# Retention, a top-1 mixture of experts and a rational feed-forward block on one core: the counts are copied sooner, the transition to the first expert and the last four blocks are written in another order

## The chip, the cores and the metric

One core of a Trainium2 chip. TensorE (PE) multiplies, and its weight loads are shown as an engine of their own (PEld); VectorE (DVE), ScalarE (ACT) and GpSimd (POOL) work element by element; SyncE (SP) and POOL issue transfers. Each engine takes its instructions in order and waits on semaphores. The metric is the device time of one execution, in microseconds (us).

## What is computed

```python
for t in range(S):                      # B=2, H=8, S=768, D=64
    state = gamma * state + k[:, :, t] (outer) v[:, :, t]
    y[:, :, t] = scale * q[:, :, t] @ state
x = y as 1536 tokens of 512
logits = x @ w_gate                     # 8 experts
e = argmax(logits); gate = softmax(logits)[e]
# tokens in order take the slots of their expert, up to its capacity (384)
y = gate * relu(x @ w1[e]) @ w2[e]      # 512 -> 1024 -> 512
h = y @ w_in                            # 512 -> 2048
g = (a0 + a1 h + a2 h^2 + a3 h^3) / (1 + |b0||h| + |b1|h^2 + 1e-6)
out = g @ w_out                         # 2048 -> 512
```

## The kernel before

**Precision.** All large products are split: an operand is a rounded high part (`whi`, `xh`, `ht[0]`, `gh`) and the rest (`wlo`, `xl`, `ht[1]`, `gl`), and a product is three matmuls: high by high, low by high, high by low. The high part of a weight is written by ACT (`split_hi`, L143), the low part by DVE (`split_lo`, L148), both on half tiles of 128x1024 whose raw form has six buffers.

**Attention** (`attention`) runs over twelve units of 128 tokens. In unit u PE computes the scores of u+1 (`scores`), the part of u's output that comes from the state (`inter`), the part from the unit itself (`intra`), the new state (`state`) and the logits of u-1 (`gate_mm`); DVE masks the scores (`mask`, tile `scm`), scales the output (`attn_xt`) and, by the tables `LO_AT` and `LO_END`, makes low parts of the first expert's weights. The units fall into two groups, 0 to 6 and 7 to 11. After a group's last unit `gate_parts`, `rank_mm`, `rank_pos` and `rank_put` find each token's expert and slot; `place_mm` (L490) then turns the tiles `pe` and `rr` by matmul into a table `tab` of token numbers by slot, from which POOL gathers rows of x (`xg`). The first group is placed in unit 10, and the first 128 rows of expert 0 are gathered there at once (`early_gather`, transposed in `early_x` as `xtp`).

**The transition** (`attn_tail`): the first layer of expert 0 on those 128 rows (`win_l1`, two halves of twelve products, both in one tile of two PSUM banks), relu by ACT (`win_relu`), transposes back (`win_turn`, tile `htp`), their high and low parts (`win_parts`, tile `ht`), and in between the second group's routing, its `place_mm` and `counts`, which copies the tokens per expert from PSUM (`off<-rk`, L499) and tests for an overfull expert. Attention's PSUM pool closes there and a new one opens: the first product of the second layer (`win_l2`, L754, in `first_expert`) waits until everything that reads the old pool is done. `first_expert` runs the second layer's 24 products with the transposes of the next 96 rows (`expert_x`, L882) after the 18th.

**Experts 1 to 7** follow in `moe`, then `ffn`: 48 steps n, each a block of 128 hidden features by 512 tokens. `ffn_a` multiplies, ACT, DVE and POOL compute the fraction (`ffn_i`, `ffn_p`, `ffn_r`, `ffn_e`), `ffn_g` splits it (low part by POOL, for n = 47 by DVE), `ffn_b` multiplies it out into four tiles m of 128 tokens. After the last of a row of blocks DVE adds the tiles to `acc` (`ffn_out`, L1122) and POOL scatters finished tiles to the output (`put_out`, L1131). `ffn_tail` writes this out for the last blocks, n = 44 to 47: one row of four tiles ends with block 43, the last one with block 47.

The order is written by hand (manual schedule): an engine's queue holds its instructions as the code calls them.

Of the kernel before, what the change touches and what calls it, by code (L numbers as in the profile page):

```python
# [34 lines left out]
WA, WC = 7, 3  # L35
LOADS = (0, 1, 0, 1, 0, 1, 0, 2, 1, 1, 1, 2)
HI_AT = {4: (0,), 5: (1,), 8: (2,), 9: (3, 4), 10: (5,)}
LO_AT = {5: (0,), 6: (1,)}
LO_END = {9: (2,), 10: (3,), 11: (4,)}
NA = 48  # L40
LOAD_AT = {1: (34, 0), 2: (34, 1), 6: (35, 0), 7: (35, 1)}
# [39 lines left out]
class Build:  # L81
# [398 lines left out]
        tt(out=pe, in0=self.over(self.col("iota"), g), in1=self.across(pm, g, 128), op=ALU.is_equal)  # L480
        self.place[b] = (pe, rr)

    def place_mm(self, b, tag="tpa"):
        nc = self.nc
        pe, rr = self.place.pop(b)
        u0, u1 = self.units(b)
        n = E * (self.nsub + 1)
        tp = self.bank(tag, "tp")[:, 0 : 2 * n]
        for i in range(u1 - u0):
            nc.tensor.matmul(tp, lhsT=pe[:, i], rhs=rr[:, i], start=(i == 0), stop=(i == u1 - u0 - 1))  # L490
        tp = tp.rearrange("p (a n) -> p a n", a=2)
        if b == 0:
            nc.vector.tensor_copy(self.tab, tp)
        else:
            nc.vector.tensor_tensor(out=self.tab, in0=self.tab, in1=tp, op=ALU.add)

    def counts(self):
        nc = self.nc
        nc.vector.tensor_copy(self.off, self.cnt)  # L499
        nc.vector.tensor_tensor(out=self.off[:, 0:1], in0=self.off[:, 0:1], in1=self.pad, op=ALU.add)  # L500
        nc.vector.tensor_reduce(out=self.ovf, in_=self.off[0:1, 0:E], axis=AX.X, op=ALU.max)
        top = float(min(W, self.cap))
        nc.vector.tensor_scalar(out=self.ovi, in0=self.ovf, scalar1=top, scalar2=None, op0=ALU.is_gt)
        nc.vector.tensor_scalar(out=self.ov, in0=self.ovf, scalar1=top, scalar2=None, op0=ALU.is_gt)
# [52 lines left out]
    def attention(self):  # L557
        nc, tc, a = self.nc, self.tc, self.a
        with ExitStack() as st:
# [42 lines left out]
            for u in range(NU):  # L602
                last = u == NU - 1
                if u + 4 < NU:
                    for c in range(2):
                        self.attn_load(u + 4, c)
                self.load_next(LOADS[u])
                if u + 2 < NU:
                    self.scale(u + 2, pool)
                if u + 3 < UPB:  # L610
                    self.y_table(u + 3, pool)
                for n in LO_AT.get(u, ()):
                    self.split_lo(n // 2, n % 2)
                if 1 < u < NU - 1:
                    self.scores(u + 1)
                    self.mask(u + 1)
                if u - 4 in done:
                    self.place_mm(done[u - 4])
                if u == UA + 3:
                    self.early_gather()  # L620
                if u - 2 in done:
                    next(gate)
                self.inter(u)
                self.intra(u)
                self.attn_xt(u)
                if u - 2 in done:
                    next(gate)
                if u == 1:
                    self.scores(2)
                    self.mask(2)  # L630
                self.state(u)
                if u == 0:
                    self.scores(1)
                    self.mask(1)
                    nc.scalar.activation(out=self.wi[:, :, 0:128], in_=ident, func=AF.Copy)
                    nc.scalar.activation(out=self.wi[:, :, 128:], in_=wg, func=AF.Copy)
                if u == 1:
                    nc.scalar.activation(out=self.tri, in_=self.col("tri"), func=AF.Copy)
                    nc.scalar.activation(out=self.b0a, in_=self.ab[:, 4:5], func=AF.Abs)
                    nc.scalar.activation(out=self.b1a, in_=self.ab[:, 5:6], func=AF.Abs)  # L640
                    nc.vector.memset(self.cq, 1.0 + 1e-6)
                if u - 2 in done and not last:
                    self.rank_mm(done[u - 2])
                if last:
                    self.early_x()
                if u:
                    self.gate_mm(u - 1)
                    self.gate_out(u - 1, (0,))
                if u - 1 in done:
                    gate = self.gate_parts(done[u - 1])  # L650
                    next(gate)
                if u:
                    self.gate_out(u - 1, (1,))
                for n in HI_AT.get(u, ()):
                    self.split_hi(n // 2, n % 2)
                if u - 2 in done and not last:
                    self.rank_pos(done[u - 2])
                if u - 3 in done and not last:
                    self.rank_put(done[u - 3])
                for n in LO_END.get(u, ()):  # L660
                    self.split_lo(n // 2, n % 2)
# [19 lines left out]
    def attn_tail(self):  # L681
        u, b = NU - 1, len(GROUPS) - 2
        self.gate_mm(u)
        ps = self.pair_bank("s", "l1").rearrange("p (a n) -> p a n", a=2)
        ps = [ps[:, 0], ps[:, 1]]
        self.early_lo()
        self.win_l1(self.x0, ps, range(0, 10))
        self.gate_group(b)
        self.gate_out(u)
        self.load_next(4)  # L690
        self.rank_mm(b)
        self.rank_pos(b)
        self.h0 = self.wp.tile([128, 2, 512], F32, tag="wt", name="h0", bufs=3)
        self.split_hi(3, 0)
        self.win_l1(self.x0, ps, range(10, 12))
        self.win_relu(ps, self.h0, 0)
        self.split_hi(3, 1)
        self.rank_put(b)
        self.win_l1(self.x0, ps, range(12, 20))
        tp = self.win_turn(self.h0, 0, self.bank("xk", "htp"))  # L700
        self.win_l1(self.x0, ps, range(20, 24))
        self.win_relu(ps, self.h0, 1)
        self.split_lo(2, 1)
        t1 = self.win_turn(self.h0, 1, self.bank("st", "htp"))
        self.place_mm(b, "lg")
        self.indices(self.gidx, E * (self.nsub + 1))
        self.ht0 = self.win_parts(tp)
        self.split_lo(3, 0)
        self.ht1 = self.win_parts(t1)
        self.split_lo(3, 1)  # L710
        self.counts()
        self.nprep = 8

    def win_l1(self, x, ps, seq):
# [75 lines left out]
    def first_expert(self):  # L790
        bank = self.bank
        acc, hts = bank("l2"), (self.ht0, self.ht1)
        seq = [(0, i) for i in (0, 3, 6, 9, 1, 4, 7, 10, 2, 5, 8, 11)]
        seq += [(1, i) for i in (0, 3, 6, 9, 1, 4, 2, 5, 8, 11, 7, 10)]
        self.win_l2(hts, acc, seq[:18], last=False)
        self.expert_x(0, 1)
        self.rows()
        self.win_l2(hts, acc, seq[18:], first=False)
        y = self.y_rows(acc, 0)
        x = [t.pop(0)[:, :, 128:W] for t in (self.xh, self.xl)]  # L800
        ps = [bank("l1")[0:W2] for _ in range(2)]
        h = self.wp.tile([128, 2, 512], F32, tag="wt", name="h1", bufs=3)[0:W2]
        self.win_l1(x, ps, range(0, 12))
        self.win_relu(ps, h, 0)
        self.x_gate(1, 0)
        self.win_l1(x, ps, range(12, 18))
        self.y_turn(y, 0)
        ht0 = self.win_split(h, 0, bank("l1"))
        self.x_gate(1, 1)
        self.win_l1(x, ps, range(18, 24))  # L810
        self.win_relu(ps, h, 1)
        self.expert_x(1, 0)
        self.gather(4)
        self.prep_next()
        acc = bank("l2")
        self.win_l2((ht0,), acc, [(0, i) for i in range(0, 6)], last=False)
        ht1 = self.win_split(h, 1, bank("l1"))
        self.win_l2((ht0,), acc, [(0, i) for i in range(6, 12)], first=False, last=False)
        self.prep_next()
        self.expert_x(1, 1)  # L820
        self.gather(5)
        for _ in range(2):
            self.prep_next()
        self.win_l2((ht0, ht1), acc, [(1, i) for i in range(12)], first=False)
        self.y0 = self.y_rows(acc, 1)
        for _ in range(2):
            self.prep_next()
        for i in range(4):
            del self.whi[i], self.wlo[i]
# [356 lines left out]
    def ffn_tail(self):  # L1186
# [6 lines left out]
        self.ffn_b([(n - 4, m) for m in range(4)])  # L1193
        self.ffn_r(n)
        self.ffn_e(n - 1)
        self.ffn_g(n - 1)
        self.ffn_out()
        self.put_outs()
        self.ffn_e(n)
        self.ffn_g(n)  # L1200
        self.ffn_b([(k, m) for k in (n - 3, n - 2) for m in range(4)])
        for m in ((n - 1, 0), (n - 1, 1), (n, 0), (n, 1)), ((n - 1, 2), (n, 2)), ((n - 1, 3), (n, 3)):
            self.ffn_b(m)
            self.ffn_out()
            self.put_outs()

# [110 lines left out]
```

## Time and profile before

| | |
|---|---|
| median of 3 runs | 524.83 us (524.3 to 525.09) |
| the profiled execution | 523.4 us, of which 521.6 us are the span from the first to the last instruction |
| PE busy | 504.5 us, 97% of the span, 3538 matmuls |
| PEld, DVE, ACT, POOL busy | 442.1, 404.4, 361.7, 244.9 us |
| PE's share of the chain that ended last | 62% |
| mean granted clock | 0.989 of full speed |

The page divides the span into 40 slices of 13 us with the busy share of each engine in tenths and the clock that was granted to PE (PEclk); the timeline lists instructions with start, duration and, in square brackets, the idle time of their engine ahead of them and what ended it. A row that merges several instructions spans them all.

### The profile page before, as it was taken

Reading aid. Unit: us, or ns where it says so; the run is one execution under the profiler, and the core shown is the slowest. Engines: PE = TensorE matmul, PEld = TensorE weight load, DVE = VectorE, ACT = ScalarE, POOL = GpSimd, SP = SyncE. Lnnn points to the kernel's source line nnn. Section 1 sums busy time; section 2 is a strip of 40 time slices with the busy share of each in tenths; the row PEclk is TensorE's granted clock in tenths of the full one; section 3 lists DMA queues with packets and bytes.
Section 4 is the critical chain, followed back from the end, with each engine's and each line's share of the span. In section 5 each row is a group of like instructions: output and inputs, shape, how many; then the busy total and the mean of one; then the engine's idle time right before and its main releaser. Section 6 shows DMA issues by size and latency. Waiting matters only on the chain.

```text
span 521.6 us, 9409 instructions
## 1 busy us (share of the span) xinstructions
PE 504.5 (97%) x3538; PEld 442.1 (85%) x3538; DVE 404.4 (78%) x577; ACT 361.7 (69%) x588; POOL 244.9 (47%) x187
## 2 busy tenths in 40 slices
PE   7999969999999999999999999999999999999994
PEld 5888747999999999999978888888888888888873
DVE  3468752887977979787496989999899998865972
ACT  1345514886685957764697989999899987776750
POOL 2531031113432548163345446775667865444765
PEclk9999989999999999999999999999999999999998
DMA  8999752789987999995220002222022200000203
GB/s 316 402 416 352 218 169 78 244 311 311 325 284 254 363 279 334 277 263 194 72 90 1 0 1 81 82 80 81 1 80 83 80 1 0 1 0 0 82 4 158
DMA packets 27266, 83.08 MB, mean 159 GB/s; under 512 B 4944, under 2 KB 5328, under 8 KB 27216
## 3 DMA queue, kind: packets, MB, share of 16 engines
q1 hardware_dynamic: 24592, 75.09, 42.6%
q0 software_dynamic: 2624, 7.35, 4.0%
q8 instruction: 28, 0.46, 0.4%
q14 instruction: 22, 0.18, 0.1%
HBM read 71.93 MB, written 10.49 MB: 158 GB/s over the span
## 4 chain that ended last, share of the span: by engine, by line
PE 62%; issue 2%; POOL 1%; ACT 1%; DVE 1%; POOLq 0%; ACTq 0%
PE h L1029 8%; PE h L1031 8%; PE h L1030 8%; PE o L1102 7%; PE o L1100 7%; PE o L1101 7%; PE l L911 3%; PE l L913 3%; PE l L912 3%; PE l L940 3%; PE l L939 3%; PE l L938 3%; POOL out L1131 1%; PE tp L882 1%; ACT fh L1060 0%
## 5 line engine op out<-in xcount | busy, mean ns | idle before, releaser
L148 DVE TENSOR_TENSOR wlo<-raw,whi 128x1024 fp32r<-128x1024 f32 x80 | 110.8, 1399 | 17.3 <-ACT whi L143 17.0
L1080 POOL TENSOR_TENSOR gg<-fx,gg 128x512 fp32r<-128x512 f32 x47 | 61.1, 1299 | 70.8 <-issue 62.9
L143 ACT ACTIVATE whi<-raw 128x1024 fp32r<-128x1024 f32 x80 | 83.1, 1053 | 3.5 <-PE l L939 3.4
L1029 PE MATMUL h<-yh,whi 128*128 128x512 f32 x192 | 74.9, 390 | 0.4 <-DVE fx L1068 0.4
L1100 PE MATMUL o<-whi,gg 128*128 128x512 f32 x192 | 74.8, 390 | 0.0
L1031 PE MATMUL h<-yh,wlo 128*128 128x512 f32 x192 | 74.8, 389 | 0.0
L1030 PE MATMUL h<-yl,whi 128*128 128x512 f32 x192 | 74.7, 389 | 0.0
L1101 PE MATMUL o<-wlo,gg 128*128 128x512 f32 x192 | 74.7, 389 | 0.0
L1102 PE MATMUL o<-whi,gg 128*128 128x512 f32 x192 | 74.7, 389 | 0.0
L1055 POOL TENSOR_TENSOR fw<-fh,fw 128x512 f32<-128x512 f32 x48 | 64.3, 1339 | 15.3 <-ACT fw L1044 14.5
L204 POOL TENSOR_TENSOR gq<-gq 128x512 int32<-128x512 int32 x16 | 26.1, 1629 | 85.9 <-DVE gq L201 68.2
L1042 ACT ACTIVATE fx<-h,ct 128x512 f32<-128x512 f32 x48 | 37.3, 777 | 39.4 <-PE h L1031 37.6
L911 PE MATMUL l<-xh,whi 128*128 128x224 f32 x224 | 62.0, 277 | 0.1
L938 PE MATMUL l<-hh,whi 128*128 128x224 f32 x224 | 61.9, 276 | 0.0
L913 PE MATMUL l<-xh,wlo 128*128 128x224 f32 x224 | 61.5, 275 | 0.0
L940 PE MATMUL l<-hh,wlo 128*128 128x224 f32 x224 | 61.5, 274 | 0.0
L912 PE MATMUL l<-xl,whi 128*128 128x224 f32 x224 | 61.5, 274 | 0.0
L939 PE MATMUL l<-hl,whi 128*128 128x224 f32 x224 | 61.4, 274 | 0.0
L1066 DVE SCALAR_TENSOR_TENSOR fw<-fw,cq,h 128x512 f32<-128x512 f32 x48 | 35.6, 741 | 10.0 <-ACT h L1061 10.0
L911 PEld LDWEIGHTS l<-xh,whi 128*128 128x128 f32 x224 | 43.0, 192 | 0.4 <-ACT yh L777 0.3
L939 PEld LDWEIGHTS l<-hl,whi 128*128 128x128 f32 x224 | 43.0, 192 | 0.1
L938 PEld LDWEIGHTS l<-hh,whi 128*128 128x128 f32 x224 | 43.0, 192 | 0.1
(161 smaller groups left out, 1184.5 us busy)
## 6 DMA issues: line engine op xcount, KB each, us to landing
raw<-wm SPq DMA_DIRECT2D x64, 512.0 KB
r<-wf SPq DMA_DIRECT2D x32, 512.0 KB
kv<-kv SPq DMA_DIRECT2D x24, 512.0 KB
wd<-gq SPq DMA_DIRECT2D x16, 256.0 KB
raw<-wd SPq DMA_DIRECT2D x8, 512.0 KB
xd<-xs SPq DMA_DIRECT2D x12, 256.0 KB
ca<-ct SPq DMA_DIRECT2D x1, 268.0 KB
xg<-xd,gidx POOLq DMA_INDIRECT x16
```

The source lines that it names most:

```text
L143: nc.scalar.activation(out=self.whi[i][:, sl], in_=raw, func=AF.Copy)
L148: (eng or self.nc.vector).tensor_tensor(out=self.wlo[i][:, sl], in0=raw, in1=self.whi[i][:, sl].bitcast(F32), op=ALU.subtract)
L911: nc.tensor.matmul(ps[:, fi], lhsT=wh[:, sl], rhs=xh[:, k], start=(k == 0), stop=False)
L912: nc.tensor.matmul(ps[:, fi], lhsT=wh[:, sl], rhs=xl[:, k], start=False, stop=False)
L938: mm(lhsT=wh[:, ws], rhs=fh, start=(f == 0 and o % 2 == 0), stop=False)
L939: mm(lhsT=wh[:, ws], rhs=fo, start=False, stop=False)
L1029: nc.tensor.matmul(h, lhsT=wh[:, sl], rhs=self.yh[:, k, ts], start=(k == 0), stop=False)
L1030: nc.tensor.matmul(h, lhsT=wh[:, sl], rhs=self.yl[:, k, ts], start=False, stop=False)
L1031: nc.tensor.matmul(h, lhsT=wl[:, sl], rhs=self.yh[:, k, ts], start=False, stop=(k == 3))
L1100: self.nc.tensor.matmul(ps, lhsT=gh[:, ms], rhs=wh[:, ws], start=first, stop=False)
L1101: self.nc.tensor.matmul(ps, lhsT=gh[:, ms], rhs=wl[:, ws], start=False, stop=False)
L1102: self.nc.tensor.matmul(ps, lhsT=gl[:, ms], rhs=wh[:, ws], start=False, stop=last)
```

## The change

No operation is added or dropped; POOL and DVE, PE and the PSUM banks meet in another order.

- Units: the low parts of the first two half tiles are made in units 6 and 7, not 5 and 6 (`LO_AT`); in unit 10 the state's part of the output (`inter`) goes ahead of `place_mm`.
- Transition: the second half of the first layer has a bank of its own (`xk`); `counts` is divided into `count` (the copy, right after `rank_put`) and `overfull`; `place_mm` moves ahead of the last four products of the first layer, into the bank pair `y`; the transposes of both halves follow each other behind these products.
- First expert: the 96 rows' transposes stand after 14 products, not 18.
- End: of the four sums and scatters of the row that ends with block 43, two sums and one scatter go ahead of block 46's split, the others between block 47's steps; the last two blocks are multiplied tile by tile.

```diff
-LO_AT = {5: (0,), 6: (1,)}
+LO_AT = {6: (0,), 7: (1,)}
...
-    def place_mm(self, b, tag="tpa"):
+    def place_mm(self, b, tp=None):
...
-        tp = self.bank(tag, "tp")[:, 0 : 2 * n]
+        tp = (self.bank("tpa", "tp") if tp is None else tp)[:, 0 : 2 * n]
...
-    def counts(self):
-        nc = self.nc
-        nc.vector.tensor_copy(self.off, self.cnt)
+    def count(self):
+        self.nc.vector.tensor_copy(self.off, self.cnt)
+
+    def overfull(self):
+        nc = self.nc
         nc.vector.tensor_tensor(out=self.off[:, 0:1], in0=self.off[:, 0:1], in1=self.pad, op=ALU.add)
...
+                if u - 2 in done:
+                    next(gate)
+                self.inter(u)
                 if u - 4 in done:
                     self.place_mm(done[u - 4])
                 if u == UA + 3:
                     self.early_gather()
-                if u - 2 in done:
-                    next(gate)
-                self.inter(u)
                 self.intra(u)
...
-        ps = self.pair_bank("s", "l1").rearrange("p (a n) -> p a n", a=2)
-        ps = [ps[:, 0], ps[:, 1]]
+        ps = [self.pair_bank("s", "l1")[:, 0:512], self.bank("xk", "l1")]
...
         self.rank_put(b)
+        self.count()
+        self.split_lo(2, 1)
         self.win_l1(self.x0, ps, range(12, 20))
-        tp = self.win_turn(self.h0, 0, self.bank("xk", "htp"))
+        self.place_mm(b, self.pair_bank("y", "tp"))
         self.win_l1(self.x0, ps, range(20, 24))
         self.win_relu(ps, self.h0, 1)
-        self.split_lo(2, 1)
+        t0 = self.win_turn(self.h0, 0, self.bank("lg", "htp"))
         t1 = self.win_turn(self.h0, 1, self.bank("st", "htp"))
-        self.place_mm(b, "lg")
         self.indices(self.gidx, E * (self.nsub + 1))
-        self.ht0 = self.win_parts(tp)
         self.split_lo(3, 0)
+        self.ht0 = self.win_parts(t0)
+        self.split_lo(3, 1)
         self.ht1 = self.win_parts(t1)
-        self.split_lo(3, 1)
-        self.counts()
+        self.overfull()
...
-        self.win_l2(hts, acc, seq[:18], last=False)
+        self.win_l2(hts, acc, seq[:14], last=False)
         self.expert_x(0, 1)
         self.rows()
-        self.win_l2(hts, acc, seq[18:], first=False)
+        self.win_l2(hts, acc, seq[14:], first=False)
...
         self.ffn_e(n - 1)
+        self.ffn_out(2)
+        self.put_out(self.outs.pop(0))
         self.ffn_g(n - 1)
-        self.ffn_out()
+        self.ffn_e(n)
+        self.ffn_out(1)
+        self.ffn_g(n)
+        self.ffn_out(1)
         self.put_outs()
-        self.ffn_e(n)
-        self.ffn_g(n)
         self.ffn_b([(k, m) for k in (n - 3, n - 2) for m in range(4)])
-        for m in ((n - 1, 0), (n - 1, 1), (n, 0), (n, 1)), ((n - 1, 2), (n, 2)), ((n - 1, 3), (n, 3)):
-            self.ffn_b(m)
+        for m in range(4):
+            self.ffn_b([(n - 1, m), (n, m)])
```

What stands in DVE's queue from the second group's `pe` on, in `attn_tail`; `wlo` are low parts of weights, `ht` the low parts of the first layer's output, `off<-rk` the copy of the counts. Before:

```order
L480 TENSOR_TENSOR pe<-ct,pm 128x640
L148 TENSOR_TENSOR wlo<-raw,whi 128x1024
L495 TENSOR_TENSOR tab<-tab,tp 128x64
L508 TENSOR_SCALAR gidx<-tab 128x32
L745 TENSOR_TENSOR ht<-htp,ht 128x512
L148 TENSOR_TENSOR wlo<-raw,whi 128x1024
L745 TENSOR_TENSOR ht<-htp,ht 128x512
L148 TENSOR_TENSOR wlo<-raw,whi 128x1024
L499 COPY off<-rk 128x16
```

and after:

```order
L480 TENSOR_TENSOR pe<-ct,pm 128x640
L498 COPY off<-rk 128x16
L148 TENSOR_TENSOR wlo<-raw,whi 128x1024
L495 TENSOR_TENSOR tab<-tab,tp 128x64
L510 TENSOR_SCALAR gidx<-tab 128x32
L148 TENSOR_TENSOR wlo<-raw,whi 128x1024
L747 TENSOR_TENSOR ht<-htp,ht 128x512
L148 TENSOR_TENSOR wlo<-raw,whi 128x1024
L747 TENSOR_TENSOR ht<-htp,ht 128x512
```

The copy went from the end of the row to its second place, and the last operation of the row that reads the old PSUM pool is now the second `ht`.

PE's queue at the same place, from the last product of the first layer's first 20 to the transposes of the next rows (`tp<-ct,xg`); `tp<-rr,pe` is `place_mm`. Before:

```order
L719 MATMUL l_889<-wlo,xh_111 128x512
L738 MATMUL htp<-ct,h_969 128x128 x4
L719 MATMUL l_889<-whi,xl_112 128x512 x4
L738 MATMUL htp<-ct,h_969 128x128 x4
L490 MATMUL tp<-rr,pe 128x64 x5
L754 MATMUL l_1057<-whi,ht 128x512 x4
L754 MATMUL l_1057<-wlo,ht 128x512 x4
L754 MATMUL l_1057<-whi,ht 128x512 x8
L754 MATMUL l_1057<-wlo,ht 128x512 x2
L882 MATMUL tp<-ct,xg 128x128 x4
```

and after:

```order
L721 MATMUL l_890<-wlo,xh_111 128x512
L490 MATMUL tp<-rr,pe 128x64 x5
L721 MATMUL l_890<-whi,xl_112 128x512 x4
L740 MATMUL htp<-ct,h_970 128x128 x8
L756 MATMUL l_1058<-whi,ht 128x512 x4
L756 MATMUL l_1058<-wlo,ht 128x512 x4
L756 MATMUL l_1058<-whi,ht 128x512 x6
L884 MATMUL tp<-ct,xg 128x128 x4
```

`place_mm` moved ahead of the last four products of the first layer and both halves' transposes stand behind them; the next rows' transposes moved four products ahead. (The trace lists ten matmuls for `place_mm`'s five.)

POOL's queue at the end, block 45's and 46's low parts (`gg`), block 47's denominator (`fw`) and the scatters (`out`). Before:

```order
L1080 TENSOR_TENSOR gg<-fx,gg 128x512
L1055 TENSOR_TENSOR fw<-fh,fw 128x512
L1080 TENSOR_TENSOR gg<-fx,gg 128x512 x2
L1131 DMA out<-acc_4022,perm 1536x512
L1131 DMA out<-acc_4024,perm 1536x512
```

and after:

```order
L1082 TENSOR_TENSOR gg<-fx,gg 128x512
L1057 TENSOR_TENSOR fw<-fh,fw 128x512
L1082 TENSOR_TENSOR gg<-fx,gg 128x512
L1133 DMA out<-acc_4023,perm 1536x512
L1082 TENSOR_TENSOR gg<-fx,gg 128x512
L1133 DMA out<-acc_4025,perm 1536x512
```

The first of the eight scatters moved ahead of block 46's low part.

## Rows read from the trace of the kernel before

**Rows 1.** The page: the granted clock in 40 slices of the span.

```profile
PEclk9999989999999999999999999999999999999998
```

**Rows 2.** Stretches: length, then PE, PEld, DVE, ACT, POOL busy, clock, DMA.

```profile
60.00:80.00 20.00, 14.21 (x75) 10.96 (x74) 11.15 (x39) 5.32 (x12) 4.43 (x4) 0.83 0.68 219
...
300.00:400.00 100.00, 100.00 (x443) 82.81 (x442) 92.73 (x130) 92.56 (x147) 65.40 (x49) 1.00 0.20 64
```

**Rows 3.** Timeline of the units: start, duration, what, idle before and its releaser.

```profile
32.51 1.16 PE L331 MATMUL sc<-kv 64*128 64x128 f32 x16 [0.32 <-DVE scm L294]
...
51.21 1.77 PE L490 MATMUL tp<-rr,pe 128*128 128x64 f32 x14 [0.51 <-DVE pe L480]
...
52.92 0.67 PE L331 MATMUL yt<-kv,s 64*64 64x128 f32 x16
...
54.03 1.20 POOL L832 DMA_INDIRECT xg<-xd,gidx  x1 [7.31 <-DVE gidx L508]
...
57.75 0.66 PE L673 MATMUL xtp<-ct,xg 128*128 128x128 f32 x4
```

**Rows 4.** Waits of the weight loads, 20 to 55 us: total, times, longest.

```profile
PEld sc L331 <- DVE scm L294: 0.8, 2, 0.5
```

**Rows 5.** A stretch behind the early gather, columns as in rows 2.

```profile
57.00:57.25 0.25, 0.25 (x10) 0.25 (x8) 0.00 (x0) 0.25 (x1) 0.00 (x0) 1.00 0.10 33
```

**Rows 6.** Timeline of the transition, 64 to 82 us.

```profile
64.66 0.50 PE L719 MATMUL l<-whi,xh 128*128 128x512 f32 x1 [0.69 <-ACT h L728]
...
65.72 0.82 DVE L480 TENSOR_TENSOR pe<-ct,pm 128x640 f32<-128x640 f32 x1
...
66.98 1.18 PE L719 MATMUL l<-whi,xl 128*128 128x512 f32 x4
...
68.84 0.66 PE L738 MATMUL htp<-ct,h 128*128 128x128 f32 x4 [0.69 <-ACT h L728]
69.34 1.23 PE L490 MATMUL tp<-rr,pe 128*128 128x64 f32 x10
69.54 0.60 ACT L744 ACTIVATE ht<-htp 128x512 fp32r<-128x512 f32 x1 [0.26 <-PE htp L738]
...
71.32 1.00 POOL L832 DMA_INDIRECT xg<-xd,gidx  x1 [16.08 <-DVE gidx L508]
71.55 1.22 DVE L148 TENSOR_TENSOR wlo<-raw,whi 128x1024 fp32r<-128x1024 f32 x1
...
72.68 0.68 DVE L745 TENSOR_TENSOR ht<-htp,ht 128x512 fp32r<-128x512 f32 x1
...
74.42 0.17 DVE L499 COPY off<-rk 128x16 f32<-128x16 f32 x1
...
74.73 2.05 PE L754 MATMUL l<-whi,ht 128*128 128x512 f32 x4 [4.17 <-DVE off L499]
...
81.35 0.60 PE L882 MATMUL tp<-ct,xg 128*128 128x128 f32 x4
```

**Rows 7.** Stretches around the lower clock, columns as in rows 2.

```profile
73.00:74.00 1.00, 0.00 (x0) 0.00 (x0) 1.00 (x2) 0.00 (x0) 0.70 (x2) 0.55 0.82 270
...
79.00:80.00 1.00, 1.00 (x4) 0.74 (x4) 0.00 (x0) 0.00 (x0) 0.00 (x0) 0.54 0.85 328
...
516.00:517.00 1.00, 0.00 (x0) 0.00 (x0) 0.00 (x0) 0.00 (x0) 0.69 (x2) 0.91 0.38 156
```

**Rows 8.** Timeline of the end.

```profile
504.10 2.48 DVE L1122 TENSOR_TENSOR acc<-o,acc 128x512 f32<-128x512 f32 x4
...
505.46 1.30 POOL L1080 TENSOR_TENSOR gg<-fx,gg 128x512 fp32r<-128x512 f32 x1 [0.83 <-ACT gg L1078]
...
509.09 0.39 PE L1100 MATMUL o<-whi,gg 128*128 128x512 f32 x1
...
514.73 0.69 DVE L1122 TENSOR_TENSOR acc<-o,acc 128x512 f32<-128x512 f32 x1 [0.67 <-PE o L1102]
...
516.39 0.98 POOL L1131 DMA_INDIRECT out<-acc,perm  x1 [0.31 <-issue]
```

## The prediction

> **What bounds the kernel now.** I first read the granted clock over the span: one slice near 70 us and the last one are below full [rows 1]. The stretches say where PE, which carries the chain, is not busy: from 300 to 400 us it works all the time, 443 matmuls in 100 us or 0.23 us each, but from 60 to 80 us it works 14.2 of 20 us, at 0.83 of the clock [rows 2]. So the span is PE's queue, and only places where PE waits, runs slow, or has already ended can give time. The timeline names them. In the units PE waits 0.32 us for a mask and 0.51 us for `pe` [rows 3]. In the transition it stands 4.17 us, until the copy of the counts is done [rows 6]; then the clock is at half, 1.2 of 2.4 GHz: 73 to 74 us has a mean of 0.55, so it fell at 73.1, and 79 to 80 has 0.54, so it rose at 79.9 [rows 7]. At the end PE is done before 514.7, but POOL issues the last scatter only at 516.39 [rows 8].
>
> **The units (0.9 us).** The first `wlo` no longer stands ahead of a mask in DVE's queue. PE gets back 0.32 us [rows 3] for certain; the weight loads show two waits for masks, 0.8 us together [rows 4], partly beside running matmuls. Between 0.3 and 0.8 I take 0.4, near PE's own row. The moved `wlo` find their high parts ready and stand between masks that DVE has time for; if it had not, the same 0.3 would return a unit later.
> `inter` now goes ahead of `place_mm`. PE's 0.51 us wait for `pe` is covered by these 0.67 us of products [rows 3], which need only the state: 0.5, or 0.25 if DVE's own chain to `pe` does not come forward with PE.
> What is late next is the early gather. Its index waits for `place_mm`, which starts only some 0.3 us sooner, while PE arrives at `xtp` 0.9 sooner than 57.75 [rows 3]. But the transfers are nearly silent from 57.0 on [rows 5], so its bytes were in about 0.7 us before they were used; 0.3 sooner, it is in at 56.7, and PE comes at 56.85. So 0.9 stands; the lower bound, a late landing signal, is 0.3.
>
> **The transition (2.1 us).** I use before's times; all of it moves forward by the 0.9. DVE ends `pe` at 65.72 + 0.82 = 66.54. With the second bank PE need not wait for the relu (0.69 at 64.66), but that gives nothing: its eight products then end at 64.66 - 0.69 + 8 x 0.23 = 65.8, and `place_mm` needs `pe`. So PE waits 0.8 us and runs `place_mm` from 66.6, 1.23 us, to 67.8, and the four products, 1.18, to 69.0. The relu, an ACT operation of 0.60, ends at 69.6; the first half's transposes run meanwhile, the second half's then take 0.66, to 70.3. There PE runs out of work.
> DVE has copied the counts (0.17), made one `wlo` (1.22, to 67.9), then the table, the index and the second `wlo`, all before 70. The first `ht` waits for ACT's high part, 69.6 + 0.60 = 70.2; then 0.68, a third `wlo` of 1.22, and the second `ht` of 0.68: 72.8. Such rows overlap by 0.1 (71.55 + 1.22 against the next start, 72.68), so 72.5. That `ht` is now the last reader of the old PSUM pool; with the 0.14 us from copy to product (74.42 + 0.17 to 74.73) PE starts the second layer at 72.65, not 74.73: 2.1 us, 1.8 without overlaps (all durations [rows 6]). The count's copy itself costs nothing now: the third `wlo` and `ht` stand where it stood, and they set the end.
> The transposes after 14 products need the gathered rows. The gather was issued 0.75 us after `place_mm` (70.57 to 71.32), so now at 68.6; PE comes at 72.65 + 14 x 0.23 = 75.9, 7.3 us later. Before it was 10.0 us (71.32 to 81.35), the early gather took at most 3.7 (54.03 to 57.75) [rows 3, 6]. I take no wait; at worst it is 2.7. Behind them ten products, 2.3 us, hide ACT's and DVE's split of those rows; before, six did, without a wait.
>
> **The clock (0.8 us).** In before PE worked at half speed from 74.73 to 79.9 [rows 6, 7], 5.2 us, which cost 2.6. The new stand is 70.3 to 72.65, 2.35 us. The clock fell 2.5 us after PE had stopped (69.34 + 1.23 = 70.6, to 73.1), and at the end of the kernel 2.1 us after the last product: 516 to 517 has 0.91, a fall at 516.8, with the last matmul over by 514.7 [rows 7, 8]. So 2.35 us is just where it falls. The gain lies between 0 (it falls and costs as much) and 2.6 (it stays). I take that it falls and costs 1.8, so 0.8: nearer to the row of before, less one third because the stand is shorter.
>
> **The end (0.65 us).** POOL had been idle 0.83 us ahead of block 46's `gg` at 505.46 [rows 8]; the first scatter takes that place, once its sum is there (504.1 + 2.48/4 = 504.7). `gg` then ends at about 507.3 instead of 506.8; PE needs it at the third product of 509.09, 509.5, so 2.2 us cover the move. Two sums are now behind block 47's three DVE operations and one on each side of its split; their banks are not needed again, and block 47's fraction is ready 1.2 us (two sums of 0.62) sooner. The products tile by tile do not change PE's end. POOL's queue then has a free place for every scatter: the last one waits for the last sum, 514.73 + 0.69 = 515.42, and with the 0.31 us that stands ahead of a transfer in its row starts at 515.7, not 516.39: 0.65, between 0.4 and 0.75. Its landing is as long as before.
>
> **The sum.** 0.9 + 2.1 + 0.8 + 0.65 = 4.45 us. The profiled execution took 523.4 us, 1.8 outside its span of 521.6; the sum makes 519.0 of it. The median is 524.83, and there I put it: 520.4. After the transition PE has no further wait that this would open: the experts' weights are fetched as their buffers come free, and these come free as much sooner.
>
> **Rivals.** *The clock stays up.* For it: PE's other waits, up to 0.69 us [rows 6], left the clock alone, and 2.35 is less than the 2.5 of before. Against it: the 2.1 us at the end. The sum is then 0.9 + 2.1 + 2.6 + 0.65 = 6.25: 518.6. The Trainium skill ("TensorE: Matmul & The Clock Gate", section "Why this matters for your kernels") says that only longer idle gaps between bursts of matmuls throw the clock back, and by that rule this rival would hold; the fall at the end of this trace speaks against leaning on it.
> *It falls for as long as before.* The half-speed stretch of 73.1 to 79.9 was 6.8 us, of which PE stood 1.6; if all 6.8 meet products they cost 3.4. Then the clock gives 0 to -0.8: 521.2 to 522.0. A wait for the gathered rows would end there too.
> *The change does not do what it says:* another reader of the old pool is as late as the copy was. Units and end remain, 1.55: 523.3. Against it: the order has no later reader than the second `ht`.
> *Slower.* PE's new wait for `pe`, 0.8 us, lowers the clock already there, ahead of `place_mm`. It decides if such a wait is enough; 0.69 was not. Then `place_mm`, four products and eight transposes, 1.23 + 1.18 + 2 x 0.66 = 3.7 us, take 3.7 more, and with the second stand behind them the half clock costs 3.4 instead of 2.6: 0.9 + 2.1 - 3.7 - 0.8 + 0.65 = -0.85, 525.7.
>
> **How the numbers follow.** Forecast 520.4 (519.5 to 521.1): 50%. Clock stays, 518.6: 31%. Longer half clock or a gather wait, 521.2 to 522.0: 12%. No effect in the transition, 523.3: 4%. Slower, 525.7: 3%. The range takes the first three with their bounds, 518.1 to 522.0, and leaves out the last two and the edges. A measurement of this kernel tells 0.2%, 1.05 us, from no change: the first three cases and most of the fourth are faster by more (0.95); the slower case at 525.7 is within it or just beyond: 0.03 same, 0.02 slower.
>
> **What would show it.** In the trace after: no wait of PE for DVE's copy, but one of about 2.4 us for the second `ht`, at 71.7 in its own time; the second layer's products 0.9 + 2.1 us sooner; a wait of about 0.8 us for `pe` ahead of `place_mm`; no wait for a mask near 32 us; `xtp` at about 56.9. The stretches tell whether the clock fell, near 72, and for how long: that alone moves the result by 2 us. At the end, one scatter ahead of `gg` and the last one 0.3 us behind the last sum. I am wrong if PE waits for the gathered rows, if POOL's `gg` comes after 509.5, or if the weights of expert 1 now come late.

## The result and the profile after

| | before | after |
|---|---|---|
| median | 524.57 us (523.14 to 526.71, 8 runs) | 519.54 us (518.2 to 522.71, 8 runs) |
| the profiled execution | 523.4 us, span 521.6 | 519.17 us, span 517.4 |
| mean granted clock of it | 0.989 | 0.999 |

The ratio is 0.9905 (95% interval 0.988 to 0.9931): 5.0 us faster, forecast 4.45. The time lies between the forecast, 520.4, and its first rival, 518.6. In the profiled execution the clock did not fall in the transition, as in the rival. The page's line of granted clock after, where before had two slices below full [rows 1]:

```profile
PEclk9999999999999999999999999999999999999999
```

The transition after (PE and POOL; start, duration, engine, line, and in brackets the wait and what ended it; rows of before are in [rows 6]):

```profile
60.96 0.48 PE L721 MATMUL l<-whi,xh 128*128 128x512 f32 x1
...
67.62 1.30 PE L490 MATMUL tp<-rr,pe 128*128 128x64 f32 x10 [0.85 <-DVE off L498]
...
70.60 0.66 PE L740 MATMUL htp<-ct,h 128*128 128x128 f32 x4 [0.25 <-ACT h L730]
73.55 1.21 PE L756 MATMUL l<-whi,ht 128*128 128x512 f32 x4 [2.29 <-DVE ht L747]
...
76.90 0.60 PE L884 MATMUL tp<-ct,xg 128*128 128x128 f32 x4
...
79.66 0.39 PE L721 MATMUL l<-whi,xh 128*96 128x512 f32 x1
```
```profile
69.31 1.22 DVE L148 TENSOR_TENSOR wlo<-raw,whi 128x1024 fp32r<-128x1024 f32 x1
...
69.68 1.73 POOL L834 DMA_INDIRECT xg<-xd,gidx  x1 [13.44 <-DVE gidx L510]
```

PE waits 0.85 us ahead of `place_mm` (the releaser shown is DVE's copy, which ends just behind `pe`), and 2.29 for the second `ht`, where before it stood 4.17 for the copy. It comes to the gathered rows 7.2 us after their issue and does not wait. The first `xk` starts 1.02 us later than in the trace of before, which has the earliest start of all fourteen traces of this document (27.16 to 28.45). The two traces at that place, at the first group's routing and (before) at three more rows that the table below starts from, before and then after:

```profile
27.16 1.19 PE L350 MATMUL xk<-wi,xt 128*128 128x136 f32 x8
42.18 0.22 DVE L387 TENSOR_TENSOR eq<-eq,ct 128x56 f32<-128x56 f32 x1
43.96 0.19 PE L422 MATMUL rk<-oh,tri 128*128 128x56 bf16 x1
...
60.01 0.48 PE L719 MATMUL l<-whi,xh 128*128 128x512 f32 x1
...
83.18 0.39 PE L719 MATMUL l<-whi,xh 128*96 128x512 f32 x1
...
514.30 0.39 PE L1102 MATMUL o<-whi,gg 128*128 128x512 f32 x1
```
```profile
28.18 1.19 PE L350 MATMUL xk<-wi,xt 128*128 128x136 f32 x8
42.48 1.07 POOL L264 TENSOR_TENSOR kv<-kv,ca 128x512 f32<-128x512 f32 x1 [3.71 <-PE sc L331]
42.68 0.94 DVE L387 TENSOR_TENSOR eq<-eq,ct 128x56 f32<-128x56 f32 x1
45.18 0.19 PE L422 MATMUL rk<-oh,tri 128*128 128x56 bf16 x1 [0.78 <-DVE oh L390]
52.45 1.77 PE L490 MATMUL tp<-rr,pe 128*128 128x64 f32 x14
58.72 0.63 PE L675 MATMUL xtp<-ct,xg 128*128 128x128 f32 x4 [0.15 <-PE yt L331]
```

Neither the wait for a mask nor that for `pe` is there any more [rows 3], but a new one of 0.78 us ahead of `rk`: DVE's `eq`, 0.22 us long before, took 0.94 while POOL worked on `kv`. The end after (before: [rows 8]):

```profile
501.53 1.00 POOL L1133 DMA_INDIRECT out<-acc,perm  x1 [0.43 <-DVE acc L1124]
502.56 1.31 POOL L1082 TENSOR_TENSOR gg<-fx,gg 128x512 fp32r<-128x512 f32 x1
...
511.19 0.69 DVE L1124 TENSOR_TENSOR acc<-o,acc 128x512 f32<-128x512 f32 x1 [0.67 <-PE o L1104]
512.16 0.98 POOL L1133 DMA_INDIRECT out<-acc,perm  x1 [0.38 <-DVE acc L1124]
```
```profile
510.77 0.39 PE L1104 MATMUL o<-whi,gg 128*128 128x512 f32 x1
```

The last scatter now starts 1.39 us after PE's last product began and waits for the last sum; before that was 516.39 - 514.30 = 2.09 us.

The 4.2 us between the two spans add up stage by stage, each as the change of a distance between two rows:

| stretch | before | after | gain |
|---|---|---|---|
| start to first `xk` | 27.16 | 28.18 | -1.02 |
| to `xtp` (units) | 30.59 | 30.54 | 0.05; without the 0.78 for `rk` 0.83 |
| to the first layer's first product | 2.26 | 2.24 | 0.02 |
| to the second layer's first product | 14.72 | 12.59 | 2.13 |
| to the first product of the 96 rows (clock) | 8.45 | 6.11 | 2.34 |
| to PE's last product | 431.12 | 431.11 | 0.01 |
| to the last scatter | 2.09 | 1.39 | 0.70 |

### The profile page after: what moved, and what is told of

It reads as the page before. It is cut to its first block, busy times and chain, and to the rows that moved or that the text cites. A ratio compares the mean times of both kernels' runs of the same rounds, so it can differ in the third digit from the quotient of the medians.

```text
span 517.4 us, 9411 instructions
## 1 busy us (share of the span) xinstructions
PE 501.7 (97%) x3538; PEld 440.0 (85%) x3538; DVE 405.0 (78%) x577; ACT 361.9 (70%) x588; POOL 245.5 (47%) x187
## 4 chain that ended last, share of the span: by engine, by line
PE 63%; DVE 2%; ACT 1%; POOL 1%; issue 1%; POOLq 0%; ACTq 0%; DVEq 0%
PE h L1031 8%; PE h L1033 8%; PE h L1032 8%; PE o L1102 7%; PE o L1104 7%; PE o L1103 7%; PE l L913 3%; PE l L915 3%; PE l L914 3%; PE l L942 3%; PE l L941 3%; PE l L940 3%; POOL out L1133 1%; PE tp L884 1%; DVE fw L1068 0%
```

## Experiments: the parts one by one

What is undecided: whether the units' part gave anything, and whether the clock is a matter of PE's stand (the time in which PE waits without work ahead of the second layer). My theory: units 0.8, transition 2.1, end 0.7 in every execution, the clock a second gain of 1.4 to 2.4 that comes in some of them. The rivals: the new wait ahead of `rk` belongs to the units' part and eats it; or the clock falls for another cause than the stand. Times of before on the chips of these runs were 523.98, 524.01 and 524.46 us. A gain in us below is what a run's ratio makes of that time; the difference of the two medians, on which the expectations below partly rest, can be up to 0.7 us more.

**Units alone.**

```diff
-LO_AT = {5: (0,), 6: (1,)}
+LO_AT = {6: (0,), 7: (1,)}
...
+                if u - 2 in done:
+                    next(gate)
+                self.inter(u)
                 if u - 4 in done:
                     self.place_mm(done[u - 4])
                 if u == UA + 3:
                     self.early_gather()
-                if u - 2 in done:
-                    next(gate)
-                self.inter(u)
```

> The kernel before with the units' part alone: the two early lower parts one unit later, and in a unit `inter` ahead of `place` and the gather. As forecast it gains 0.9 us (about 523.7): no mask wait at unit 4, no wait for `pe` ahead of `place`. The rival that the trace after suggests: the masks, now sooner on VectorE, move the gate's small operations under GpSimd's `kv` (L264), one of them (`eq`, L387) takes 0.9 instead of 0.2 us, PE waits 0.8 for `oh` ahead of `rk`, and nothing is left of the gain (about 524.6).

522.93 us (521.99 to 523.98); ratio 0.9985 (0.9974 to 0.9997), 0.8 us. PE in its trace:

```profile
27.76 1.19 PE L350 MATMUL xk<-wi,xt 128*128 128x136 f32 x8
...
44.03 0.19 PE L422 MATMUL rk<-oh,tri 128*128 128x56 bf16 x1
...
57.54 0.63 PE L673 MATMUL xtp<-ct,xg 128*128 128x128 f32 x4 [0.23 <-DMA xg<-xd,gidx]
...
74.50 2.04 PE L754 MATMUL l<-whi,ht 128*128 128x512 f32 x4 [4.17 <-DVE off L499]
...
81.97 0.39 PE L719 MATMUL l<-whi,xh 128*96 128x512 f32 x1
```

From `xk` to `xtp` it is 29.78 us, 0.81 less than before, and there is no wait ahead of `rk`: the units' part does what was forecast and does not bring that wait. Five of the six traces of kernels without this part have the wait (0.30 to 0.81 us), and three of the eight with it (0.46 to 0.78), so the change does not bring it; whether the part makes it rarer is not shown. A long `eq` (0.94 to 0.96) goes with it in three of these eight; what makes it in the other five is open. What the part did not give is the last tenth: PE now waits 0.23 us for the early gather's rows.

**Transition alone** (its part of the change whole, of which these lines are the core).

```diff
         self.rank_put(b)
+        self.count()
+        self.split_lo(2, 1)
         self.win_l1(self.x0, ps, range(12, 20))
...
+        self.place_mm(b, self.pair_bank("y", "tp"))
         self.win_l1(self.x0, ps, range(20, 24))
...
-        self.win_l2(hts, acc, seq[:18], last=False)
+        self.win_l2(hts, acc, seq[:14], last=False)
```

> The kernel before with the transition's part alone (counts copied behind `rank_put`, order of lower parts, products and `place`, 14 products ahead of the gathered rows). As forecast 2.1 us from the wait and 0.8 from the clock: 521.7. If the clock stays up, 2.1 and 2.6: about 519.9, with a mean granted clock of 0.999. If it falls in some executions and not in others, both sums show side by side, the low mean clock at the long spans.

521.58 us (519.81 to 523.07); ratio 0.9961 (0.9943 to 0.9979), 2.0 us. All 7 executions have a mean clock of 0.989 to 0.995. PE's rows, and the stretches of this kernel and of the changed one (busy time of PE, PEld, DVE, ACT, POOL with instructions, granted clock, DMA share, GB/s):

```profile
73.37 1.72 PE L756 MATMUL l<-whi,ht 128*128 128x512 f32 x4 [2.29 <-DVE ht L747]
...
81.05 0.39 PE L721 MATMUL l<-whi,xh 128*96 128x512 f32 x1
```
```profile
70.00:82.00 12.00, 9.45 (x39) 7.21 (x38) 5.34 (x19) 2.63 (x5) 6.27 (x5) 0.86 0.70 234
```
```profile
70.00:82.00 12.00, 9.46 (x47) 7.16 (x45) 5.51 (x19) 2.81 (x5) 6.46 (x5) 1.00 0.72 236
```

The stand is the same 2.29 us as in the changed kernel, but here the clock fell in it, and the 24 products and four transposes behind it take 7.68 instead of 6.11 us. From the first layer's first product (60.79) to the second's it is 12.58 us, 2.14 less than before. So the wait is worth its 2.1 us, and with this stand the clock goes either way.

**End alone** (`ffn_tail` of the change).

```diff
+        self.ffn_out(2)
+        self.put_out(self.outs.pop(0))
         self.ffn_g(n - 1)
-        self.ffn_out()
-        self.put_outs()
         self.ffn_e(n)
+        self.ffn_out(1)
         self.ffn_g(n)
+        self.ffn_out(1)
+        self.put_outs()
```

> The kernel before with the end's part alone (sums and scatters of the last blocks between the fractions, last products tile by tile). As forecast 0.65 us, about 523.9, by last scatter against last product; the trace of the changed kernel gives 0.70. The rival: the `gg` that now stand behind scatters and sums come too late for PE's last products and give the gain back: 524.6.

523.53 us (522.01 to 524.41); ratio 0.9989 (0.9978 to 0.9999), 0.6 us; the interval only just leaves out no change. The last scatter starts 1.40 us behind the last product's start, as in the changed kernel:

```profile
515.83 0.39 PE L1102 MATMUL o<-whi,gg 128*128 128x512 f32 x1
```
```profile
517.23 0.98 POOL L1131 DMA_INDIRECT out<-acc,perm  x1 [0.38 <-DVE acc L1122]
```

So 0.7 in the trace and 0.6 in the times; the rival of a late `gg` is out, since from the 96 rows' first product to the last one PE takes 431.10 us here, as in both columns of the table above.

**Transition and end, without the units** (in the changed kernel, with `inter` and the gate's step back behind `place_mm`).

```diff
-LO_AT = {6: (0,), 7: (1,)}
+LO_AT = {5: (0,), 6: (1,)}
```

> The changed kernel with the units' part undone: transition and end alone. If the three parts simply add up as they measured one by one (units 1.05, transition 2.4, end 0.45), it is 2.85 under the kernel before: about 521.1. If the transition with the end is what lets the clock stay up in half of the executions, and the units' part only its own 0.9: about 520.2.

520.6 us (520.18 to 521.35); ratio 0.9939 (0.9927 to 0.9951), 3.2 us, between both expectations. One of its 6 executions has a mean clock of 0.999, the others 0.993 to 0.995. This trace shows when the clock goes down:

```profile
73.29 1.21 PE L756 MATMUL l<-whi,ht 128*128 128x512 f32 x4 [2.29 <-DVE ht L747]
...
80.98 0.39 PE L721 MATMUL l<-whi,xh 128*96 128x512 f32 x1
```
```profile
73.00:74.00 1.00, 0.71 (x3) 0.61 (x4) 0.66 (x5) 0.00 (x0) 0.69 (x2) 1.00 0.89 324
74.00:75.00 1.00, 1.00 (x5) 0.81 (x4) 0.00 (x0) 0.00 (x0) 0.81 (x1) 0.70 0.68 213
75.00:77.00 2.00, 2.00 (x6) 1.51 (x6) 0.00 (x0) 0.00 (x0) 1.00 (x1) 0.50 0.93 326
77.00:78.00 1.00, 1.00 (x5) 0.76 (x4) 0.00 (x0) 0.00 (x0) 0.00 (x0) 0.60 0.90 270
```

The first four products ran at the full 2.4 GHz; the clock fell to 1.2 at 74.4, when PE had been at work again for 1.1 us, and rose at 77.8.

**The changed kernel once more**, with no edit.

> The changed kernel once more, beside the others: 519.5, 0.99 of the kernel before. If the sum of the three parts measured one by one (3.9 us) were all there is, it is 520.1; if the clock, up in half of the executions only with all parts together, is worth the rest, 519.2 to 519.6, and the mean clocks again fall into a group at 0.999 and one below.

519.1 us (518.27 to 521.99); ratio 0.9912 (0.9883 to 0.9942), 4.6 us. The stand is 2.29 us and the clock stays full in its trace too. Of the 14 executions of the changed kernel, 7 have a mean clock of 0.998 or 0.999, with spans of 516.4 to 517.5 us; 7 lie at 0.987 to 0.996, with 517.3 to 520.9. The lower means can come from a fall behind PE's last product, which costs nothing (a version below has 0.996 with a full clock from 60 to 82 us), so this is a count of means, not of falls. In the two slowest executions there must have been an earlier fall: means of 0.987 and 0.990 over 520.9 and 520.2 us are 13.5 and 10.4 us at half clock, and the stretch behind PE's last product has some 6.2 (511.16 to 517.4). Without the units it was 1 of 13. The parts alone add to 0.8 + 2.0 + 0.6 = 3.4 us (3.9 by the medians), all together gave 5.0 and 4.6; the intervals still overlap, so that the parts help each other by way of the clock is likely but not shown.

## Experiments: the copy and the clock

**The copy alone, moved behind `rank_put` in the kernel before.**

```diff
+    def count(self):
+        self.nc.vector.tensor_copy(self.off, self.cnt)
...
-        nc.vector.tensor_copy(self.off, self.cnt)
...
         self.rank_put(b)
+        self.count()
```

> The kernel before with one line moved: the copy of the counts right behind `rank_put`, all else in the old order. The last reader of the old PSUM pool is then the second `ht` (72.68 to 73.36 in the trace of before), and PE starts the second layer at about 73.5 instead of 74.73: 1.25 us, 522.75, with a stand of 2.9 us that still lets the clock fall. If the shorter stand kept the clock up in most executions: 520.5 to 521.5. If another reader holds PE: 524.0.

522.97 us (521.22 to 524.12); ratio 0.9974 (0.9959 to 0.9989), 1.4 us. PE now waits for the second `ht`, 1.22 us less than 4.17 [rows 6], and the clock still falls (0.86 from 70 to 82 us):

```profile
75.05 2.04 PE L757 MATMUL l<-whi,ht 128*128 128x512 f32 x4 [2.95 <-DVE ht L748]
```

So of the 2.1 us, 1.2 are this one line, which takes a lower part (1.22 us) and the copy from in front of PE; the new order of products and transposes gives the other 0.9.

**Fillers in the stand of the kernel before.** Just ahead of the first `win_parts`:

```diff
+        fp = self.pair_bank("y", "wp")[:, 0:512]
+        for _ in range(18):
+            rhs = self.wu.unsqueeze(1).to_broadcast([128, 4, 128])
+            self.nc.tensor.matmul(fp, lhsT=self.wu, rhs=rhs, start=True, stop=True)
         self.ht0 = self.win_parts(tp)
```

> The kernel before, with 18 extra matrix products (bf16, 128x512, their result used by nothing) on PE in the wait of 4.17 us ahead of the second layer. They take nothing from the wait. If a PE that stands is what makes the clock fall there, the clock now stays up and the clock's price can be read by itself: 2.6 us by the rows before, about 522.0, mean clock 0.999 instead of 0.989. If the fall has another cause, or costs less than the 0.8 that the forecast took, the time is 523.8 to 524.6.

522.56 us (521.65 to 523.79); ratio 0.9977 (0.9967 to 0.9988), 1.2 us, from products that nobody uses. The clock no longer falls:

```profile
71.96 4.05 PE L710 MATMUL wp<-wu 128*128 128x512 bf16 x18
76.29 1.17 PE L758 MATMUL l<-whi,ht 128*128 128x512 f32 x4 [0.28 <-DVE off L499]
...
82.33 0.39 PE L723 MATMUL l<-whi,xh 128*96 128x512 f32 x1
```
```profile
70.00:82.00 12.00, 11.32 (x59) 7.98 (x60) 4.68 (x12) 1.93 (x4) 5.08 (x5) 1.00 0.65 211
```

This shows that the standing PE is the cause here: the wait itself is as before (PE is released by `off`), only PE does not stand in it. And it gives the price. From the second layer's first product to the 96 rows the same order takes 6.04 us here, 8.45 in the trace of before (clock 0.72 from 70 to 82 us) and 7.47 with the units alone (0.86). So a fall costs 1.4 or 2.4 us, by the execution, and 1.2 at the mean of 12 executions, not the 2.6 that I had read from one.

**Fillers in the stand of the changed kernel** (nine instead of 18, ahead of the same call).

> The changed kernel with 9 extra matrix products (bf16, 128x512, results used by nothing) on PE in the wait of 2.29 us that is left ahead of the second layer. If the changed kernel's longer executions are those in which the clock falls in that wait, all are now like the short ones: about 518.7 against 519.5 without them, and 5.3 us under the kernel before. If the spread of its executions has another cause (the start, VectorE beside GpSimd), nothing changes: 519.0 to 519.6.

519.5 us (518.48 to 520.12); ratio 0.9912 (0.9898 to 0.9926), the same as without. All 5 mean clocks are 0.997 to 0.999, and in the trace the clock is full from 70 to 82 us, so falls are gone as expected, but the median is not the 518.7 expected of a full clock. Its profiled execution lost 0.94 us in an expert far behind, where PE waited for a scaled `xg`; the changed kernel's trace has no such wait, but five executions do not settle whether that is chance. What falls cost the changed kernel at its median is thus not shown.

```profile
216.45 0.66 PE L888 MATMUL tp<-ct,xg 128*128 128x128 f32 x4 [0.94 <-ACT xg L878]
```

**A longer stand.** The third lower part of the transition is made twice, ahead of the second `ht`.

```diff
+        raw = self.raw[3, 1]
+        self.split_lo(3, 1)
+        self.raw[3, 1] = raw
         self.split_lo(3, 1)
         self.ht1 = self.win_parts(t1)
```

> The changed kernel with the third lower part of the transition made twice, 1.22 us more for VectorE ahead of the second `ht`, so that PE stands 3.5 instead of 2.29 us. If the wait and the clock add, it is 1.2 us for the wait, and as the clock now falls in every execution, 0.5 to 1.2 us more at the median: 521.2 to 522.0. If the clock were no matter of that wait: 520.7.

522.0 us (520.66 to 523.69); ratio 0.9955 (0.9938 to 0.9972). That is 2.3 us above the changed kernel on the same chip by the ratios, and 2.9 by the medians. PE stands 1.26 us longer, all 12 mean clocks are 0.989 to 0.996, and in the trace the clock is at 0.86 from 70 to 82 us:

```profile
73.50 2.05 PE L759 MATMUL l<-whi,ht 128*128 128x512 f32 x4 [3.55 <-DVE ht L750]
```

So 1.2 us of work on another engine cost 2.3 to 2.9 us; the rest fits the clock, since the products behind the stand take 7.66 us in this trace, not 6.11. In the traces with stands of 2.95, 3.55 and 4.17 us the clock fell every time (five traces), in those with 2.29 in two of four.

## Experiments: a version that beats both

The stand that is left is no need of the data: the first product reads the first `ht`, done at 71.76 in the changed kernel's trace, 1.8 us before PE begins:

```profile
71.07 0.69 DVE L747 TENSOR_TENSOR ht<-htp,ht 128x512 fp32r<-128x512 f32 x1 [0.54 <-ACT ht L746]
```

It waits for the second because the new PSUM pool begins when all of the old is read. With a pool for each bank, both in the attention and behind it, each bank's first user waits for that bank alone:

```diff
-            self.pm, self.turn = self.pool("pa", space=PSUM, stack=st), {}
+            self.pm = {t: self.pool(f"p{t}", space=PSUM, stack=st) for t in ("b0", "s", "b3", "y", "b6", "b7")}
+            self.turn = {}
...
-            self.pm = self.pool("pm", space=PSUM)
+            self.pm = {f"b{i}": self.pool(f"q{i}", space=PSUM) for i in range(8)}
...
-        self.win_l2(hts, acc, seq[:14], last=False)
+        self.win_l2(hts, acc, seq[:22], last=False)
...
-        self.win_l2(hts, acc, seq[14:], first=False)
+        self.win_l2(hts, acc, seq[22:], first=False)
```

> The changed kernel with one PSUM pool for each bank in place of one for the attention and one for what follows, so that the second layer's first product waits for its own bank alone and no longer for the second `ht`; the gathered rows are turned behind 22 products instead of 14. PE should begin the second layer at about 71.3 instead of 73.55 (own time of the changed kernel's trace) and reach the gathered rows as they land (76.9): `l<-whi,xh` of the next rows at 78.3 instead of 79.66, 1.35 us, and no wait left in which the clock can fall: about 518.0. The rival: the rows land later than that, beside the lower parts, and the wait only moves there: 519.5.

517.07 us (516.59 to 517.87); ratio 0.987 (0.9855 to 0.9885), 0.9 us less than expected. The trace shows 0.7 of it: the rows had landed when PE came to them, at 76.30, and the 96 rows' first product starts at 77.61, not 78.3. PE begins the second layer right behind the transposes:

```profile
70.67 0.66 PE L744 MATMUL htp<-ct,h 128*128 128x128 f32 x4 [0.25 <-ACT h L734]
71.16 1.19 PE L760 MATMUL l<-whi,ht 128*128 128x512 f32 x4
```

**The same with late lower parts**, and 20 products ahead of the rows.

```diff
-        self.split_lo(3, 0)
         self.ht0 = self.win_parts(t0)
-        self.split_lo(3, 1)
+        self.split_lo(3, 0)
         self.ht1 = self.win_parts(t1)
+        self.split_lo(3, 1)
```

> As the one with a pool for each bank, with both lower parts of the last slot behind the first and the second `ht` on VectorE, and the gathered rows behind 20 products. The gather's issue on GpSimd then has no lower part beside it: 1.0 instead of 1.73 us, and the rows land 0.7 us sooner: about 517.3. The rival: the lower part of the product (1, 1), now done at about 73.0, and the last one at 74.9, come too late for PE, and nothing is gained on the former: 518.0 or more.

515.92 us (515.02 to 516.7); ratio 0.9846 (0.9832 to 0.9859), better than both expectations; no product waits for a lower part, and the 96 rows begin at 76.55. From the first layer's first product that is 16.18 us (60.37 to 76.55), against 16.58 in the version before (61.03 to 77.61). So the edit shows as 0.4 us in the traces; the trace of the version before also has a wait of 0.64 us for `pe` in the units, which this one lacks, and what more the times show is open. The gather's first issue with no lower part beside it, the second, and the third, which begins beside a moved lower part (71.09, 1.22 us):

```profile
69.10 1.00 POOL L838 DMA_INDIRECT xg<-xd,gidx  x1 [13.43 <-DVE gidx L513]
70.41 1.00 POOL L838 DMA_INDIRECT xg<-xd,gidx  x1 [0.30 <-issue]
71.71 1.46 POOL L838 DMA_INDIRECT xg<-xd,gidx  x1 [0.30 <-issue]
```

**And with `place_mm` behind the whole first layer**, and 22 products ahead of the rows.

```diff
-        self.place_mm(b, self.pair_bank("y", "tp"))
         self.win_l1(self.x0, ps, range(20, 24))
         self.win_relu(ps, self.h0, 1)
+        self.place_mm(b, self.pair_bank("y", "tp"))
```

> As the one with a pool for each bank and late lower parts (515.9), with `place` behind all of the first layer instead of 4 products ahead of its end, and the gathered rows behind 22 products. PE's wait of 0.85 us for `pe` is filled by those 4 products (0.93 us) and the wait of 0.25 for the relu goes: up to 0.9 us, about 515.1. The rival: the rows are then the limit, since the gather starts 0.1 us later and PE comes 0.4 us sooner: 515.5 to 515.9.

515.34 us (514.87 to 517.15); ratio 0.9836 (0.981 to 0.9861). The waits for `pe` and for the relu are gone, and one of 0.25 for the first `ht` has come:

```profile
66.42 1.30 PE L493 MATMUL tp<-rr,pe 128*128 128x64 f32 x10
67.56 1.04 PE L744 MATMUL htp<-ct,h 128*128 128x128 f32 x8
68.85 1.19 PE L760 MATMUL l<-whi,ht 128*128 128x512 f32 x4 [0.25 <-ACT ht L750]
```

The last two differ by less than their intervals; both beat the changed kernel by 3 to 4 us. Neither has a stand left ahead of the second layer; the first still waits 0.85 us for `pe` and 0.25 for the relu.

## Why the prediction was right, and where it was off

- **Units, 0.9.** Size nearly right: 0.81 us between the same rows in the kernel with this part alone, 0.8 in its times. The step that was off is the landing of the early gather: I took the transfers' silence after 57.0 us [rows 5] for the rows being there; PE waits 0.23 us for them. The profiled execution shows none of this gain, since the later start (1.02) and the wait behind the long `eq` (0.78) hide it; both vary between traces, with and without this part.
- **Transition, 2.1.** Right in size and in its steps: 0.85 us of wait ahead of `place_mm` (0.8 forecast), a stand of 2.29 for the second `ht` (2.35), 2.13 us gained to the first product, and no wait for the rows at 7.2 us after their issue. The rival that the change would not do what it says is out, as is the one where the 0.8 us wait lowers the clock.
- **The clock, 0.8.** This term was mis-sized. I took that the clock falls and costs 1.8 us of before's 2.6. At the same stand of 2.29 us the traces show both outcomes: it held in both of the changed kernel and fell in both of the kernels without the units' part. That it fell in some executions of the changed kernel too follows for the slowest two from their mean clocks (0.987, 0.990). What it costs when it falls is 1.4 to 1.6 us (2.4 in the longer falls), 1.2 at the mean in the kernel before. In the pair of profiled executions the term was 2.34. A median of 519.54, between the two cases, would fit a mixture of both, but the fillers, with the clock full in all means, gained nothing on it, so this is not shown. That the sum came out near is in part luck: in the profiled pair the clock gave 1.5 us more than forecast, and start and units 1.9 less. By the rule of the Trainium skill ("TensorE: Matmul & The Clock Gate", section "Why this matters for your kernels") a gap as short as this one should leave the clock alone; the changed kernel's two traces agree, the two without the units' part, 7.68 and 7.69 us for the same products, do not.
- **The end, 0.65.** 0.70 in the changed kernel and with this part alone. One scatter stands ahead of `gg`, and the last one starts 0.28 us behind the last sum's end (511.19 + 0.69), for the forecast's 0.31.
- **The range**, 518.1 to 522.0, was made by the clock alone. The clock is not all that moves the executions: those with fillers, all at a mean of 0.997 or more, lie between 518.48 and 520.12.

What stays open: why the clock holds through 2.29 us in some executions and not in others, and whether the units' part makes that likelier. What PE did ahead of the stand does not tell them apart: in all four traces it was eight transposes (69.75 to 71.26 in the changed kernel's), and no run took these away to see whether they have a part in it.

## What to carry to other kernels

Look at what a wait on a new pool really waits for: a single small copy, or a tile of another bank, can hold an engine that has its data. Price a fall of the clock from several executions, and test it with fillers in the wait: here 1.2 us came back without touching the wait. And before shortening a wait by reordering, ask whether it is there for the data at all; a pool for each bank removed what the reordering had only halved.

## What the runs showed of the hardware that I had not expected

- The clock can fall after PE is back at work: at 74.4 us, 1.1 us behind the first product at 73.29 that ended the stand, and it stayed at 1.2 GHz for 3.4 us although PE was busy all the time.
- DVE and POOL can hold each other up: a DVE operation on 128x56 elements took 0.94 instead of 0.22 us beside POOL's `kv`, and POOL's gather issue 1.73 instead of 1.00 us beside a DVE lower part (69.31, 1.22 us). With that lower part moved, the issue took 1.00, and a later one beside it 1.46. The Trainium skill ("SBUF — State Buffer", section "SBUF: two separate sides") says that a DVE operation with two SBUF inputs and a GpSimd one that reads SBUF share a port pair that the first holds for its whole length; the rows of `eq` and `kv` agree: `kv` began first and ended at 43.55, the long `eq` at 43.62. Not every overlap does it: in the kernel before, a lower part began at 71.55 inside the gather's issue of 71.32, and with 1.22 and 1.00 us neither took longer [rows 6].
